# Second expert's output product in seven products for the three middle token blocks

## The chip, the core and the metric

The kernel runs on one core of a Trainium2 chip. The metric is the device time of one execution in microseconds (us).

## What is computed

Attention with a decay over 4 x 8 heads (576 tokens, 64 wide), then two experts, one after the other, on all 2304 tokens of width 512. The change lies in the last line of the second expert.

```python
def _moe2_ref(x, w_gate, w_val, w_out):          # x: 2304 x 512
    gate = 1.0 / (1.0 + np.exp(-(x @ w_gate)))   # w_gate, w_val: 512 x 1536
    val = x @ w_val
    return (gate * val @ w_out).astype(np.float32)   # w_out: 1536 x 512
```

## The kernel before

Every matrix is held as two float16 halves, a high and a low one, and a product A B is three matmuls on TensorE: high x high, high x low, low x high, summed in float32 in PSUM.

The second expert works on blocks of tokens, `XB` (L376): four of 512 and one of 256. Within a block there are six units (`units`, NJ = 6), each for 256 of the 1536 hidden columns. A unit does the following, all in `gv_stream` (L1379), which issues the TensorE work in a fixed order written out by hand.

- Gate and value together are one matrix product with seven products instead of eight, the form of Strassen and Winograd. `product` (L1356) issues one of them: 12 matmuls of half a block, 256 columns (128 in the last block). Four PSUM banks A, B, C, D hold the sums. `copy` (L1373) has ScalarE carry the running sum of A over to B, then to C, then to D.
- VectorE and ScalarE turn the banks into z = gate x value: `tanh`, `value2`, `first` and `second` (L1450 to L1481). `z_pair` (L1483) writes z in two float16 halves into a tile `zz`. The units' z comes in two float32 tiles, `t1` (two token quarters) and `v2`.
- The output product of unit u is `out_parts(u)` (L1493): one part for each 128 tokens, 6 matmuls of 512 columns. The parts are put into four slots of unit u + 1 (`some(slot)`, L1407): slot 0 after product t3, slot 1 after b21, slot 2 after t4, slot 3 after b22. They sum over the six units of the block in four PSUM banks (`o_acc`), and `store` (L1531) scales each to SBUF on ScalarE and sends it out.

The weights come as 64-bit floats. `conv` (L1298) loads and converts them to float32 on VectorE, `group` (L1241) makes the sums for the seven products, and `pair` and `out_pair` split them in halves. `sums(blk)` (L1312) makes the four sums of the token matrix that the seven products need. All this runs while the first expert ends and block 0 of the second one runs.

The order on each engine comes from the planner `Order` (L60). Each task is a generator that yields the engine and an estimate of the time; the planner issues the earliest that can start, and among those ready the one with the smallest due time. `take` and `give` hand out buffers, `need` waits for events. `scaled`, `rest` and `add` let the planner pick among VectorE, ScalarE and GpSimd. N1 = 72 is the number of the first expert's steps; unit u is due at N1 + 2.7 u.

Of the kernel before, what the change touches and what calls it, by code (L numbers as in the profile page):

```python
# [59 lines left out]
class Order:  # L60
# [242 lines left out]
def t_dve(cols):  # L303
    return cols * 1.04e-3 + 0.066
# [15 lines left out]
def attention_moe_moe_kernel(ctx, tc, qk, v, f, carry, ident, const, rows_q, rows_k, w_in, w_out, w_gate, w_val, w_out2, out):  # L320
# [26 lines left out]
        "d": 3, "r": 2, "g": 4, "e": 2,  # L347
        "sp": 4, "pp": 3, "pt": 5, "stage": 4, "vt": 4, "sm": 6, "low": 2, "q": NQ,
        "wr": 3, "wf": 2, "wr2": 2, "wf2": 6,
    }  # L350
# [19 lines left out]
    def t_g(name):  # L370
        return mt.tile([128, 2, 512], FP16, tag="g", name=name, bufs=BUFS["g"])
# [9 lines left out]
    def words(t, o, n):  # L381
        return t.rearrange("p a b c -> p (a b c)")[:, o:o + n]
# [793 lines left out]


    w2, f2, zz_t, s_t = {}, {}, {}, {}
    GDUE = 19.133
    GGAP = 2.2  # L1180
    NJ = NG2
# [16 lines left out]
    def w2_stream():  # L1198
        yield from need(*[("x", NB - 1, p, 1) for p in range(NPB)])
        done("att")  # L1200
        od.fill = None
        att.close()
        pool = ctx.enter_context(tc.tile_pool(name="w2", bufs=1))
        s_pool.append(pool)
        s0 = pool.tile([128, 4, 2, 512], FP16, name="s0")
        s_t[0] = [s0[:, i] for i in range(4)]

        old = [(t, key, g) for g in range(NG1) for t, key in ((win[g], "in"), (wout[g], "out"))]
# [24 lines left out]
        s_t[1] = [place("s1") for i in range(4)]  # L1233
        spawn(sums(0), N1 - GDUE)
        for j in range(NJ):
            where = {free[k] for k in free if k[1] == j and k != "s1"}
            spawn(group(j, pool, 6 * j, where), N1 - GDUE + GGAP * j)

    PIECES = ("b11", "t1", "b22", "t3", "t2", "b21", "t4")

# [51 lines left out]
    def out_pair(j, a, where):  # L1292
# [2 lines left out]
        yield from pair(w2["o", j][a], f2[f][0], S_WO2, ("w", "o", j, a))  # L1295
        give("wf2", f2[f][1])

    def conv(pool, src, key, n):  # L1298
        (ri,) = yield from take("wr2", turn=("wr2", n))
        raw = pool.tile([128, 512, 2], I32, tag="wr", name="wraw", bufs=BUFS["wr2"])  # L1300
# [5 lines left out]
        w = pool.tile([128, 512], I32, tag="wf", name="wf", bufs=BUFS["wf2"])  # L1306
        yield from float32(w, raw)
        give("wr2", ri)
        f2[key] = w.bitcast(FP32), fi
        done(key)  # L1310

    def sums(blk):  # L1312

        half = XB[blk] // 2
        n = 2 * half
        x = xt[blk]
        yield from need(*[("y", bb, h) for bb in range(2 * blk, 2 * blk + n // 256) for h in range(2)])
        if blk == 1:
# [7 lines left out]
        fis = yield from take(*["wf2"] * 4, turn=("wf2", blk and 6 * NJ + blk))  # L1326
        for q, fi in zip(("21", "22", "11", "12"), fis):
            w = s_pool[0].tile([128, 512], I32, tag="wf", name="af", bufs=BUFS["wf2"]).bitcast(FP32)[:, 0:n]
# [12 lines left out]
            if q == "12":  # L1341
                yield from add(f["12"][0], f["12"][0], f["11"][0], ALU.subtract, n)
                spawn(s_pair(s[3], f["12"][0], n, ("s", blk, 4)), due)
        for i, q in ((3, "21"), (2, "11"), (1, "22"), (4, "12")):
            yield from need(("s", blk, i))
            give("wf2", f[q][1])
# [7 lines left out]
    s_pool = []  # L1354

    def product(bank, piece, j, x, half, start):  # L1356

# [21 lines left out]
    def gv_stream():  # L1379
# [8 lines left out]
        outs = iter(())  # L1388
        for u, (blk, j) in enumerate(units):
            od.due(N1 + 2.7 * u)  # L1390
            done(("step", N1 + u))
            half = XB[blk] // 2
            n = 2 * half
            A, B, C, D = (t[:, 0:n] for t in banks)
            ntt = XB[units[u - 1][0]] // 128 if u else 0
# [10 lines left out]

            def some(slot):  # L1407

                if 4 - slot <= ntt:
                    part = next(outs, None)  # L1410
                    if part is not None:
                        yield from part()
# [27 lines left out]
            yield from need(("ad", u), ("s", blk, 4))  # L1440
            yield from product(D, "b22", j, s[3], half, False)
            spawn(first(u, t1, di, D, n), N1 + 2.7 * u - 30)
            if j == NJ - 1:
                done(("used", blk))
            yield from some(3)
            outs = iter(out_parts(u))
        for part in outs:
            yield from part()

    def tanh(u, t1, B):  # L1450

# [10 lines left out]
    def first(u, t1, di, D, n):  # L1462
        yield from need(("t", u))
        yield "DVE", t_dve(n)
        nc.vector.scalar_tensor_tensor(t1, t1, 1.0, D, op0=ALU.add, op1=ALU.mult)
        done(("z", u))
        yield from z_pair(u, 0, t1, n)
        give("d", di)

    def second(u, v2, ri, C, e, ei, n):  # L1470
        yield from need(("v", u))
        yield "DVE", t_dve(n)
        nc.vector.tensor_tensor(e, C, e, op=ALU.add)
        done(("g", u))
        yield "ACT", t_act(n), "exp"
        nc.scalar.activation(out=e, in_=e, func=ACTF.Tanh, scale=0.5 / (S_Y * S_GT))
        yield "DVE", t_dve(n), "port"
        nc.vector.scalar_tensor_tensor(v2, e, 1.0, v2, op0=ALU.add, op1=ALU.mult)
        give("e", ei)
        yield from z_pair(u, 1, v2, n)  # L1480
        give("r", ri)  # L1481

    def z_pair(u, h, z, n):  # L1483
        (gi,) = yield from take("g")
        zz = t_g("zz")
        yield from scaled(zz[:, 0, 0:n], z, S_ZS, n)
        yield from rest(zz[:, 1, 0:n], z, S_ZS, zz[:, 0, 0:n], n)
        zz_t[u, h] = (zz, gi)
        done(("zz", u, h))

    o_acc = {}
# [1 line left out]
    def out_parts(u):  # L1493
# [5 lines left out]
        def part(tt):  # L1499
# [4 lines left out]
            zz, gi = zz_t[u, h]  # L1504
            if j == 0:
                tag = f"acc{tt}" if tt < 2 else "s"
                (ai,) = yield from take(tag)
# [8 lines left out]
                nc.tensor.matmul(dst, lhsT=zh, rhs=w[:, 1], start=False, stop=False)  # L1516
                nc.tensor.matmul(dst, lhsT=zl, rhs=w[:, 0], start=False, stop=(j == NJ - 1 and ff == 1))  # L1517
            if t == ntt // 2 - 1:
                give("g", gi)
# [178 lines left out]
```

## Time and profile before

| | us |
|---|---|
| median of 3 runs | 927.55 |
| lowest and highest | 927.09, 931.93 |
| profiled execution | 930.57 |
| its span, first to last instruction | 928.8 |
| TensorE busy | 906.6 (98%) |
| VectorE busy | 628.1 (68%) |
| ScalarE busy | 520.0 (56%) |

Times in the rows are in us from the start of the span, and a duration named "mean ns" is in nanoseconds. Matmuls are pipelined: the listed duration of one reaches over the start of the next, so the pace is read from start to start. PE is TensorE (PEld its weight loads), DVE VectorE, ACT ScalarE, POOL GpSimd, SP the engine that issues most DMAs.

### The profile page before, as it was taken

To read this page: it belongs to the slowest core of one execution; us is meant where nothing else is said; L and a number is where in the kernel's file an instruction comes from. 1 tells how busy PE (TensorE), PEld (TensorE's weight loads), DVE (VectorE), ACT (ScalarE), POOL (GpSimd) and SP (SyncE) were. 2 spreads that over 40 slices of the span, in tenths; PEclk is the share of its full clock that TensorE was granted. 3 is DMA by queue.
4 is the path that set the end of the run, shared out by engine and by line. 5 is a ranking of instruction groups with operands and counts; after the bars stand their busy time and mean duration, and the time that the engine had idled before them with its cause. 6 is when DMAs were issued, how large, how long until landed. Compare 5 with 4: busy or idle time off the path is not lost.

```text
span 928.8 us, 20902 instructions
## 1 busy us (share of the span) xinstructions
PE 906.6 (98%) x8583; PEld 716.1 (77%) x8583; DVE 628.1 (68%) x1483; ACT 520.0 (56%) x994; POOL 34.6 (4%) x45
## 2 busy tenths in 40 slices
PE   8979989999999999999999999999999999999998
PEld 5647778787888878878888887777777777777776
DVE  6999988786768757787799999963236243442343
ACT  4768768897777769688444454544224322422232
POOL 0000100101000101000110000000000000000000
PEclk7979999999999999999999999999999999999999
DMA  8687995759457584546344443100000000100000
GB/s 234 163 210 200 231 230 142 132 115 182 99 111 125 107 172 88 114 81 109 103 141 138 154 137 114 46 13 35 2 1 35 13 1 1 47 1 1 13 35 24
DMA packets 145713, 90.50 MB, mean 97 GB/s; under 512 B 103657, under 2 KB 127681, under 8 KB 145616
## 3 DMA queue, kind: packets, MB, share of 16 engines
q1 hardware_dynamic: 144754, 87.85, 39.4%
q8 instruction: 67, 1.10, 0.5%
q10 hardware_dynamic: 864, 1.32, 0.4%
q14 instruction: 28, 0.23, 0.1%
HBM read 50.79 MB, written 4.84 MB: 60 GB/s over the span
## 4 chain that ended last, share of the span: by engine, by line
PE 75%; DVE 11%; ACT 5%; DMA 5%; SPq 2%; issue 2%; POOL 0%; ACTq 0%; POOLq 0%; DVEq 0%
PE bank L1369 9%; PE bank L1371 9%; PE bank L1370 9%; PE o_acc L1517 5%; PE o_acc L1516 5%; PE o_acc L1515 5%; PE y_ps L1131 5%; PE y_ps L1133 5%; PE y_ps L1132 5%; PE h_ps L1081 4%; PE h_ps L1083 4%; PE h_ps L1082 4%; PE o_ps L990 2%; DVE pp L731 2%; DMA pt<-pp 2%
## 5 line engine op out<-in xcount | busy, mean ns | idle before, releaser
L1131 PE MATMUL y_ps<-g,wout 128*128 128x256 f16 x576 | 157.3, 273 | 3.6 <-DVE xt L1163 2.1
L1082 PE MATMUL h_ps<-xt,win 128*128 128x256 f16 x576 | 156.9, 272 | 0.7 <-DVE sm L748 0.7
L1081 PE MATMUL h_ps<-xt,win 128*128 128x256 f16 x576 | 157.2, 273 | 0.2 <-DVE g L1054 0.2
L1132 PE MATMUL y_ps<-g,wout 128*128 128x256 f16 x576 | 157.0, 272 | 0.4 <-DVE wout L535 0.4
L1133 PE MATMUL y_ps<-g,wout 128*128 128x256 f16 x576 | 157.0, 272 | 0.0
L1083 PE MATMUL h_ps<-xt,win 128*128 128x256 f16 x576 | 156.9, 272 | 0.0
L1459 DVE TENSOR_TENSOR v<-bank,e 128x512 f32<-128x512 f32 (+1 forms) x30 | 19.1, 637 | 163.8 <-ACT bank L1376 163.6
L1376 ACT ACTIVATE bank<-bank 128x512 f32<-128x512 f32 (+1 forms) x90 | 48.5, 539 | 136.4 <-PE bank L1371 136.2
L731 DVE SCALAR_TENSOR_TENSOR pp<-sp,sm,pp 128x384 f16<-128x384 f32 (+4 forms) x128 | 78.3, 624 | 7.4 <-ACT pp L516 6.1
L723 DVE CUSTOM_DVE_ANT_0 sp<-s_ps,mask 128x384 f32<-128x384 f32 (+4 forms) x144 | 67.6, 492 | 16.6 <-PE s_ps L858 15.9
L873 ACT ACTIVATE sp<-sp,sm 128x384 f32<-128x384 f32 (+3 forms) x112 | 63.7, 569 | 20.8 <-DVE sm L723 19.8
L1081 PEld LDWEIGHTS <-win 128*128 128x128 f16 x576 | 56.3, 98 | 12.4 <-issue 1.4
L1132 PEld LDWEIGHTS <-wout 128*128 128x128 f16 x576 | 56.3, 98 | 12.2 <-issue 4.1
L1131 PEld LDWEIGHTS <-wout 128*128 128x128 f16 x576 | 56.3, 98 | 11.1 <-issue 2.0
L1082 PEld LDWEIGHTS <-win 128*128 128x128 f16 x576 | 56.3, 98 | 9.6 <-issue 1.3
L1083 PEld LDWEIGHTS <-win 128*128 128x128 f16 x576 | 56.3, 98 | 7.5 <-issue 0.8
L1133 PEld LDWEIGHTS <-wout 128*128 128x128 f16 x576 | 56.3, 98 | 6.6
L1054 DVE SCALAR_TENSOR_TENSOR g<-h_ps,g 128x512 f16<-128x512 f32 x72 | 48.9, 685 | 11.9 <-ACT g L1050 11.6
L1044 ACT ACTIVATE h_ps<-h_ps 128x512 f32<-128x512 f32 x72 | 41.7, 584 | 16.1 <-PE h_ps L1083 15.4
L990 PEld LDWEIGHTS <-vt 128*64 128x64 f16 x1368 | 36.3, 112 | 16.5 <-issue 13.2
L990 PE MATMUL o_ps<-pt,vt 128*64 128x128 f16 (+1 forms) x1368 | 44.8, 216 | 3.1 <-DMA pt<-pp 3.1
L516 ACT ACTIVATE pp<-sp,sm 128x384 f16<-128x384 f32 (+4 forms) x64 | 40.5, 644 | 9.5 <-ACT sp L873 3.0
(207 smaller groups left out, 2268.2 us busy)
## 6 DMA issues: line engine op xcount, KB each, us to landing
xt<-w_out SPq DMA_DIRECT2D x16, 512.0 KB
xt<-w_in SPq DMA_DIRECT2D x12, 512.0 KB
wraw<-w_gate SPq DMA_DIRECT2D x12, 512.0 KB
wraw<-w_val SPq DMA_DIRECT2D x12, 512.0 KB
wraw<-w_out SPq DMA_DIRECT2D x12, 512.0 KB
out<-ob SPq DMA_DIRECT2D x16, 256.0 KB
vst<-v SPq DMA_DIRECT2D x12, 320.0 KB
st<-qk SPq DMA_DIRECT2D x12, 320.0 KB
```

The lines of the kernel that those rows point to most:

```text
L723: nc.vector.tensor_tensor_reduce(out=sp, in0=ps_ap, in1=mk, op0=ALU.add, op1=ALU.min, scale=-0.125, scalar=1.0e38, accum_out=mn,)
L731: nc.vector.scalar_tensor_tensor(lo, a, scale, hi, op0=ALU.mult, op1=ALU.subtract)
L990: nc.tensor.matmul(o_ps[64 * hh:64 * hh + 64, col:col + n], lhsT=vv[:, jc, vl, 64 * hh:64 * hh + 64], rhs=ptt[:, k, q0:q0 + n], start=(jc ...
L1081: nc.tensor.matmul(dst, lhsT=wh, rhs=xh, start=(k == 0), stop=False)
L1082: nc.tensor.matmul(dst, lhsT=wh, rhs=xl, start=False, stop=False)
L1083: nc.tensor.matmul(dst, lhsT=wl, rhs=xh, start=False, stop=(k == KD - 1))
L1131: nc.tensor.matmul(dst, lhsT=wh, rhs=gh, start=first, stop=False, skip_group_check=True)
L1132: nc.tensor.matmul(dst, lhsT=wl, rhs=gh, start=False, stop=False, skip_group_check=True)
L1133: nc.tensor.matmul(dst, lhsT=wh, rhs=gl, start=False, stop=last, skip_group_check=True)
L1369: nc.tensor.matmul(dst, lhsT=wh, rhs=xh[:, k], start=first, stop=False, skip_group_check=True)
L1370: nc.tensor.matmul(dst, lhsT=wh, rhs=xl[:, k], start=False, stop=False, skip_group_check=True)
L1371: nc.tensor.matmul(dst, lhsT=wl, rhs=xh[:, k], start=False, stop=last, skip_group_check=True)
```

## The change

In blocks 1, 2 and 3 the output product is made for two units at a time, and in seven products instead of eight (Strassen and Winograd again). For one unit z is cut into 2 x 2 pieces (256 tokens by 128 hidden columns) and the output weights into 2 x 2 pieces (128 by 256). Each of the seven products is 12 matmuls of 256 columns: two units, two tiles of 128 tokens, three matmuls.

- `pieces` and `piece` make the eight pieces of a unit's z in float16 halves (A11, A12, A22 and the sums S1 to S4; A11 and A12 share a tile), in place of `z_pair`.
- `out_sums` makes the four sums of the weights (T1 to T4) of each unit in block 1. For the first four units T3 is written over the piece B12, which is first stored to DRAM (`b12_d`) and loaded back by `back` for block 4.
- `chain` issues the seven products p1, p7, p6, p2, p5, p4, p3 in seven slots: slots 1 to 3 of the unit after the pair, and slots 0 to 3 of the next. Four PSUM banks hold them; `copy` carries bank 0 to banks 1, 2 and 3 on ScalarE. `total` adds a bank to a float32 sum in SBUF, laid in the token tile of the block before, and with the block's last pair sends it out.
- Blocks 0 and 4 keep `out_parts`. In block 4 the parts of its units 0 and 1 move to its unit 2.
- `sums` of blocks 1 and up, and `out_sums`, wait until all weights are converted (`converted`). Buffers of the conversion become named slices (`f_t`, `raw_t`, `slots`).

The core of the diff:

```diff
+    def out_sums(j):
+        yield from converted()
+        w0, w1 = w2["o", j]
+        b12 = w0[:, :, 256:512]
+        if j < NSAVE:
+            yield "SP", 0.5, 128 * 1024
+            nc.sync.dma_start(out=b12_d[j], in_=b12)
+            done(("saved", j))
+        ia, ib = yield from take("wf3", "wf3")
+        f1, f2_ = (f_t[i % BUFS["wf3"]].bitcast(FP32) for i in (ia, ib))
+        yield from add(f1, w0[:, 0], w0[:, 1], ALU.add, 512)
+        yield from add(f2_, w1[:, 0], w1[:, 1], ALU.add, 512)
+        (a, b), (c, d) = ((f[:, 0:256], f[:, 256:512]) for f in (f1, f2_))
+        yield from add(a, b, a, ALU.subtract, 256)
+        yield from add(b, d, b, ALU.subtract, 256)
+        yield from add(d, d, a, ALU.subtract, 256)
+        yield from add(c, c, d, ALU.subtract, 256)
+        t = t_t[j]
+        if j < NSAVE:
+            yield from need(("part", j))
+            yield from pair2(b12, b, 1.0, 256)
+            yield from pair2(t[:, 0], a, 1.0, 256)
...
+    def pair2(dst, a, scale, n, *keys):
+        yield from scaled(dst[:, 0], a, scale, n)
+        yield "DVE", t_dve(n), "port"
+        nc.vector.scalar_tensor_tensor(dst[:, 1], a, scale, dst[:, 0], op0=ALU.mult, op1=ALU.subtract)
+        done(*keys)
...
+                if u < late:
+                    where = [(u + 1, k) for k in range(4)]
+                elif u < late + 2:
+                    where = [(late + 2, 2 * (u - late) + k) for k in range(2)]
+                else:
+                    where = [(u + 1, k) for k in (2, 3)]
+                at_slots(out_parts(u), *where)
+            elif j % 2:
+                at_slots(chain(u - 1, u), *[(u + 1, k) for k in (1, 2, 3)], *[(u + 2, k) for k in range(4)])
...
+    def pieces(u, t1, di, v2, ri):
...
+        yield from pair2(zz_t[u, "A22"][0], v2[:, 256:512], S_ZS, 256, ("zA22", u))
+        yield from need(("zt", u))
...
+        yield from pair2(za, t1, S_ZS, 512, ("zA11", u), ("zA12", u))
+        (a, b), (c, d) = ((f[:, 0:256], f[:, 256:512]) for f in (t1, v2))
+        yield from add(d, c, d, ALU.add, 256)
+        yield from add(c, a, c, ALU.subtract, 256)
+        yield from add(a, d, a, ALU.subtract, 256)
+        spawn(piece(u, v2, "S3", "S1", 0, 2, ("r", ri)), od.cur["due"])
+        yield from add(b, b, a, ALU.subtract, 256)
+        yield from piece(u, t1, "S2", "S4", 5, 7, ("d", di))
...
+        def product7(x, w, k, start):
+            bank = o_bank[k]
+            for u in us:
+                yield from after(("z" + x, u))
+                yield from need(("T", u % NJ))
+                z, buf = zz_t[u, x]
+                wp = wt[u % NJ][w]
+                yield "PE", t_pe(6, 256)
+                for t in range(2):
+                    dst = bank[:, t * 256:t * 256 + 256]
+                    zh, zl = (z[:, a, t * 128:t * 128 + 128] for a in range(2))
+                    first, last = start and u == u0 and t == 0, u == u1
+                    nc.tensor.matmul(dst, lhsT=zh, rhs=wp[:, 0], start=first, stop=False, skip_group_check=True)
+                    nc.tensor.matmul(dst, lhsT=zh, rhs=wp[:, 1], start=False, stop=False, skip_group_check=True)
+                    nc.tensor.matmul(dst, lhsT=zl, rhs=wp[:, 0], start=False, stop=last, skip_group_check=True)
...
+        def total(r, k, keys, done_, new=False, full=False):
+            yield from need(*keys)
+            if new:
+                yield "ACT", t_act(512, 0.05)
+                nc.scalar.activation(out=acc[:, r], in_=o_bank[k], func=ACTF.Copy, scale=1.0 / S_O)
+            else:
+                yield "DVE", t_dve(512)
+                nc.vector.scalar_tensor_tensor(
+                    acc[:, r], o_bank[k], 1.0 / S_O, acc[:, r], op0=ALU.mult, op1=ALU.add
+                )
...
+        def p1():
...
+            yield from product7("A11", "B11", 0, True)
+            spawn(copy(o_bank[1], o_bank[0], [("bank", 1, u0 - 1)], ("oab", u1)), -100)
+        def p7():
+            yield from need(("bank", 3, u0 - 1))
+            yield from product7("S3", "T3", 3, True)
+            done(("t3", u1))
+            tot(3, 3, (), (("ode", u1),), new=begin)
+            tot(2, 3, (), (("odf", u1),), new=begin)
...
+    def back(j):
+        yield from need(("t3", (len(XB) - 2) * NJ + j // 2 * 2 + 1))
+        yield "SP", 0.5, 128 * 1024
+        nc.sync.dma_start(out=w2["o", j][0][:, :, 256:512], in_=b12_d[j])
+        done(("back", j))
```

p6, p2, p5, p4 and p3 follow the same pattern: S2 T2 on bank 0, A12 B21 on bank 1, S1 T1 on bank 0, A22 T4 on bank 2, S4 B22 on bank 3; six totals in all for a pair.

## Rows read from the trace of the kernel before

**Rows 1.** The page: the span, and busy time of each engine

```profile
span 928.8 us, 20902 instructions
PE 906.6 (98%) x8583; PEld 716.1 (77%) x8583; DVE 628.1 (68%) x1483; ACT 520.0 (56%) x994; POOL 34.6 (4%) x45
```

**Rows 2.** View by windows: stretch, its length, each engine's busy us, granted clock, DMA

```profile
528.50:546.00 17.50, 17.50 (x160) 15.40 (x158) 17.08 (x31) 10.69 (x18) 0.00 (x0) 1.00 0.45 148
546.05:876.13 330.08, 330.08 (x2487) 243.05 (x2484) 164.46 (x274) 118.50 (x204) 1.04 (x1) 1.00 0.08 27
876.13:925.02 48.89, 48.89 (x601) 37.45 (x599) 20.14 (x52) 16.49 (x41) 0.00 (x0) 1.00 0.06 23
...
540.00:560.00 20.00, 20.00 (x164) 15.82 (x163) 19.59 (x35) 12.74 (x21) 0.00 (x0) 1.00 0.41 133
```

**Rows 3.** Timeline, TensorE, first matmuls in units 1 and 2: start us, duration us

```profile
546.05 0.27 PE L1369 MATMUL bank<-xt,b 128*128 128x256 f16 x1
...
547.36 0.27 PE L1369 MATMUL bank<-s,t 128*128 128x256 f16 x1
...
548.67 0.38 PE L1515 MATMUL o_acc<-wo,zz 128*128 128x512 f16 x1
...
549.96 0.27 PE L1369 MATMUL bank<-s,t 128*128 128x256 f16 x1
...
560.40 0.27 PE L1369 MATMUL bank<-xt,b 128*128 128x256 f16 x1
```

**Rows 4.** Weight loads by line, 610 to 876 us: count, busy us, mean ns

```profile
L1516 PEld LDWEIGHTS <-zz 128*128 128x128 f16 x150 | 14.7, 98 | 9.7
```

**Rows 5.** Timeline, block 4, first matmuls of its second unit's products 2, 3, 4

```profile
886.67 0.22 PE L1369 MATMUL bank<-s,t 128*128 128x128 f16 x1
...
887.34 0.22 PE L1369 MATMUL bank<-s,t 128*128 128x128 f16 x1
...
888.01 0.22 PE L1369 MATMUL bank<-xt,b 128*128 128x128 f16 x1
```

**Rows 6.** Groups by line, 610 to 876 us: count, busy us, mean ns, idle before

```profile
L1376 ACT ACTIVATE bank<-bank 128x512 f32<-128x512 f32 x55 | 32.0, 582 | 115.1 <-PE bank L1371 115.1
L516 ACT ACTIVATE zz<-v 128x512 f16<-128x512 f32 x5 | 3.2, 630 | 2.3 <-DVE v L1478 2.3
L535 DVE SCALAR_TENSOR_TENSOR zz<-v,zz 128x512 f16<-128x512 f32 x19 | 13.1, 691 | 0.5
L519 DVE TENSOR_SCALAR zz<-v 128x512 f16<-128x512 f32 x14 | 6.0, 427 | 0.5
L1189 DVE TENSOR_TENSOR af<-af 128x256 f32<-128x256 f32 x3 | 1.3, 423 | 0.1
L1189 POOL TENSOR_TENSOR af<-af 128x256 f32<-128x256 f32 x1 | 1.0, 1038 | 322.7 <-DVE af L1189 322.7
```

**Rows 7.** Timeline, unit 0 (no output parts): products 2 and 3, and ScalarE

```profile
530.87 0.27 PE L1369 MATMUL bank<-s,t 128*128 128x256 f16 x1
...
531.13 0.63 ACT L516 ACTIVATE wout<-wf 128x512 f16<-128x512 f32 x1 [2.41 <-DVE wf L659]
...
531.67 0.58 ACT L1376 ACTIVATE bank<-bank 128x512 f32<-128x512 f32 x1
...
532.30 0.27 PE L1369 MATMUL bank<-s,t 128*128 128x256 f16 x1
```

**Rows 8.** Timeline, two VectorE operations of 512 columns, one behind the other

```profile
688.62 0.69 DVE L535 SCALAR_TENSOR_TENSOR zz<-v,zz 128x512 f16<-128x512 f32 x1
689.22 0.68 DVE L1465 SCALAR_TENSOR_TENSOR t<-t,bank 128x512 f32<-128x512 f32 x1
```

**Rows 9.** Timeline, VectorE: the last weight conversion and the first of block 1's sums

```profile
596.05 0.69 DVE L1195 SCALAR_TENSOR_TENSOR wout<-wf,wout 128x512 f16<-128x512 f32 x1
...
596.65 0.69 DVE L1189 TENSOR_TENSOR af<-xt 128x512 f32<-128x512 f16 x1
```

More of the change, by code (lines that the diff above doesn't have):

```diff
@@ L1233, in w2_stream @@
         s_t[1] = [place("s1") for i in range(4)]
+        z22.append(place("z22"))
+        z22.append(free["z22"])
         spawn(sums(0), N1 - GDUE)
         for j in range(NJ):
-            where = {free[k] for k in free if k[1] == j and k != "s1"}
+            where = {free[k] for k in free if k[1] == j and k not in ("s1", "z22")}
             spawn(group(j, pool, 6 * j, where), N1 - GDUE + GGAP * j)
+        for j in range(NJ):
+            spawn(out_sums(j), N1 + 2.7 * (NJ + j) - TDUE)
     PIECES = ("b11", "t1", "b22", "t3", "t2", "b21", "t4")
@@ L1387, in gv_stream, with at_slots @@
         done(*[(k, -1) for k in ("ab", "ad", "t", "z", "g", "v")])
-        outs = iter(())
+        plan = {}
+        for j in range(NSAVE):
+            spawn(back(j), N1 + 2.7 * ((len(XB) - 2) * NJ + j + 3))
+        def at_slots(parts, *where):
+            for part, k in zip(parts, where):
+                plan.setdefault(k, []).append(part)
         for u, (blk, j) in enumerate(units):
@@ L1407, in some @@
             def some(slot):
[L1409 to L1412, printed above, removed]
+                for part in plan.pop((u, slot), ()):
+                    yield from part()
             yield from need(("v", u - 1), ("ad", u - 1))
@@ L1445, in gv_stream @@
             yield from some(3)
-            outs = iter(out_parts(u))
-        for part in outs:
-            yield from part()
+            if u == NJ - 1:
+                spawn(grab(), -100)
+            if not in_seven(u):
+                late = len(units) - NJ
+                if u < late:
+                    where = [(u + 1, k) for k in range(4)]
+                elif u < late + 2:
+                    where = [(late + 2, 2 * (u - late) + k) for k in range(2)]
+                else:
+                    where = [(u + 1, k) for k in (2, 3)]
+                at_slots(out_parts(u), *where)
+            elif j % 2:
+                at_slots(chain(u - 1, u), *[(u + 1, k) for k in (1, 2, 3)], *[(u + 2, k) for k in range(4)])
@@ new lines, in gv_stream, with in_seven, grab @@
+        for k in sorted(plan):
+            for part in plan[k]:
+                yield from part()
+    def in_seven(u):
+        return 0 < units[u][0] and XB[units[u][0]] == 512
+    def grab():
+        yield from need(("zz", NJ - 1, 0), ("zz", NJ - 1, 1))
+        yield from take(*["g"] * 4)
+        zp["A1"] = [t_g("za") for i in range(3)]
+        zp["A22"] = [t[:, :, k:k + 256] for t in (z22[0], t_g("zb")) for k in (0, 256)]
+        done("grab")
+    def pieces(u, t1, di, v2, ri):
+        yield from need(("zv", u), z22[1], "grab")
+        (i,) = yield from take("A22")
+        zz_t[u, "A22"] = zp["A22"][i % BUFS["A22"]], ("A22", i)
+        yield from pair2(zz_t[u, "A22"][0], v2[:, 256:512], S_ZS, 256, ("zA22", u))
+        yield from need(("zt", u))
+        (i,) = yield from take("A1")
+        za = zp["A1"][i % BUFS["A1"]]
+        zz_t[u, "A11"] = za[:, :, 0:256], ()
+        zz_t[u, "A12"] = za[:, :, 256:512], ("A1", i)
+        yield from pair2(za, t1, S_ZS, 512, ("zA11", u), ("zA12", u))
[6 more added lines that the diff above has]
+        yield from piece(u, t1, "S2", "S4", 5, 7, ("d", di))
@@ new lines, in piece, with chain, tot, p6 @@
+    def piece(u, f, p, q, kp, kq, buf):
+        ip, iq = yield from take(p, q)
+        i, k = kp + ip % BUFS[p], kq + iq % BUFS[q]
+        zz_t[u, p] = slots[0][:, i], (p, ip)
+        zz_t[u, q] = slots[0][:, k], (q, iq)
+        dst = slots[0][:, i:k + 1:k - i].rearrange("p i a n -> p a i n")
+        yield from pair2(dst, f.rearrange("p (i n) -> p i n", i=2), S_ZS, 512, ("z" + p, u), ("z" + q, u))
+        give(*buf)
+    def chain(u0, u1):
+        us = (u0, u1)
+        blk = units[u0][0]
+        begin, end = u0 % NJ == 0, u1 % NJ == NJ - 1
+        acc = words(xt[blk - 1], 0, 4096).bitcast(FP32).rearrange("p (r n) -> p r n", r=4)
+        def product7(x, w, k, start):
[13 more added lines that the diff above has]
+                    nc.tensor.matmul(dst, lhsT=zl, rhs=wp[:, 0], start=False, stop=last, skip_group_check=True)
+                if buf:
+                    give(*buf)
+        def total(r, k, keys, done_, new=False, full=False):
[3 more added lines that the diff above has]
+                nc.scalar.activation(out=acc[:, r], in_=o_bank[k], func=ACTF.Copy, scale=1.0 / S_O)
+            else:
+                yield "DVE", t_dve(512)
+                nc.vector.scalar_tensor_tensor(
+                    acc[:, r], o_bank[k], 1.0 / S_O, acc[:, r], op0=ALU.mult, op1=ALU.add
+                )
+            done(*done_)
+            if full and end:
+                t0 = blk * 512 + 256 * (r // 2)
+                yield "SP", 0.5, 128 * 2048
+                nc.sync.dma_start(
+                    out=out[t0:t0 + 256, 256 * (r % 2):256 * (r % 2) + 256].rearrange("(a p) n -> p a n", p=128),
+                    in_=acc[:, r].rearrange("p (a n) -> p a n", a=2),
+                )
+        def tot(*a, **k):
+            spawn(total(*a, **k), -100)
+        def p1():
+            if "tag" not in o_bank:
+                tags = ("acc0", "acc1", "s", "s")
+                ais = yield from take(*tags)
+                o_bank.update(enumerate(t_ps(tag, "o_bank") for tag in tags))
+                o_bank["tag"] = list(zip(tags, ais))
+                done(*[("bank", k, u0 - 1) for k in range(4)], ("oad", u0 - 1))
+            yield from need(("bank", 0, u0 - 1), ("oad", u0 - 1))
+            yield from product7("A11", "B11", 0, True)
[6 more added lines that the diff above has]
+            tot(2, 3, (), (("odf", u1),), new=begin)
+        def p6():
+            yield from need(("oab", u1))
+            yield from product7("S2", "T2", 0, False)
+            spawn(copy(o_bank[2], o_bank[0], [("bank", 2, u0 - 1)], ("oac", u1)), -100)
+        def p2():
+            yield from product7("A12", "B21", 1, False)
+            tot(0, 1, (), (("bank", 1, u1),), new=begin, full=True)
+        def p5():
+            yield from need(("oac", u1))
+            yield from product7("S1", "T1", 0, False)
+            spawn(copy(o_bank[3], o_bank[0], [("ode", u1), ("odf", u1)], ("oad", u1)), -100)
+            tot(3, 0, [("ode", u1)], (("bank", 0, u1),), full=True)
+        def p4():
+            yield from product7("A22", "T4", 2, False)
+            tot(2, 2, [("odf", u1)], (("bank", 2, u1),), full=True)
+        def p3():
+            yield from need(("oad", u1))
+            yield from product7("S4", "B22", 3, False)
+            tot(1, 3, (), (("bank", 3, u1),), new=begin, full=True)
+            if end and units[u1 + 1][0] == len(XB) - 1:
+                spawn(release(u1), -100)
+        return [p1, p7, p6, p2, p5, p4, p3]
@@ L1450, in tanh, with release @@
+    o_bank = {}
+    def release(u):
+        for k, (tag, ai) in enumerate(o_bank["tag"]):
+            yield from need(("bank", k, u), ("oad", u))
+            give(tag, ai)
+    def back(j):
[3 more added lines that the diff above has]
+        done(("back", j))
     def tanh(u, t1, B):
@@ L1465, in first @@
         nc.vector.scalar_tensor_tensor(t1, t1, 1.0, D, op0=ALU.add, op1=ALU.mult)
-        done(("z", u))
-        yield from z_pair(u, 0, t1, n)
-        give("d", di)
+        done(("z", u), ("zt", u))
+        if not in_seven(u):
+            yield from z_pair(u, 0, t1, n)
+            give("d", di)
     def second(u, v2, ri, C, e, ei, n):
@@ L1479, in second @@
         give("e", ei)
-        yield from z_pair(u, 1, v2, n)
-        give("r", ri)
+        done(("zv", u))
+        if not in_seven(u):
+            yield from z_pair(u, 1, v2, n)
+            give("r", ri)
     def z_pair(u, h, z, n):
-        (gi,) = yield from take("g")
-        zz = t_g("zz")
+        if u < NJ:
+            (gi,) = yield from take("g")
+            zz, buf = t_g("zz"), ("g", gi)
+        else:
+            tag, k = (("S4", 7), ("S1", 2))[h]
+            (gi,) = yield from take(tag)
+            zz, buf = slots[0][:, k + gi % BUFS[tag]], (tag, gi)
         yield from scaled(zz[:, 0, 0:n], z, S_ZS, n)
         yield from rest(zz[:, 1, 0:n], z, S_ZS, zz[:, 0, 0:n], n)
-        zz_t[u, h] = (zz, gi)
+        zz_t[u, h] = (zz, buf)
         done(("zz", u, h))
@@ L1503, in part @@
             yield from need(("w", "o", j, 0), ("w", "o", j, 1))
-            zz, gi = zz_t[u, h]
+            if blk and j < NSAVE:
+                yield from need(("back", j))
+            zz, buf = zz_t[u, h]
             if j == 0:
@@ L1518, in part @@
             if t == ntt // 2 - 1:
-                give("g", gi)
+                give(*buf)
+            if blk == 0 and tt == ntt // 2 - 1:
+                done(("part", j))
             if j == NJ - 1:
```

49 lines of the change are left out of this document (41 added, 8 removed).

## The prediction

> **What bounds the kernel now.** I read the page first: one engine fills the span, TensorE, with VectorE far behind it [rows 1]. A share over the whole span mixes stages, so next I cut the second expert out with the view by windows. From the first product of its first unit to its last output matmul TensorE is busy for every microsecond of each stretch, at a granted clock of 1.00 (the 2.4 GHz level), while VectorE has about half of the middle stretch free [rows 2]. The view of TensorE's waits has no entry at all after 500 us. So in this stage a microsecond of matmul time taken away is a microsecond of run time, as long as what feeds TensorE keeps up. The change takes matmuls away here and nowhere else, so the question is pace and supply.
>
> The pace comes from the timeline of TensorE [rows 3]. A gate or value product (12 matmuls of 256 columns) goes from 546.05 to 547.36, 1.31 us, or 0.109 us for each matmul. An output part (6 matmuls of 512 columns) goes from 548.67 to 549.96, 1.29 us; over a unit the parts come to 1.295 on average: 560.40 - 546.05 = 14.35 us for seven products and four parts, and (14.35 - 7 x 1.31) / 4 = 1.295. The listed duration of a matmul (0.27, 0.38) is not its price; start to start is.
>
> **The change, part by part.**
>
> **Matmuls.** By the diff a pair of units in blocks 1 to 3 gives up 8 parts and gets 7 products, each 2 units x 2 token tiles x 3 = 12 matmuls of 256 columns. Removed: 8 x 1.295 = 10.36 us. Added: 7 x 1.31 = 9.17 us. That is 1.19 us a pair, and with nine pairs 10.7 us. Blocks 0 and 4 keep their parts; only their places move, so they cost the same.
>
> **Weight loads.** Each 256-column matmul still has a load of its own: 84 in a pair where there were 48. A load takes 98 ns [rows 4], less than the 109 ns of the matmul that covers it, and the same alternation runs at 0.109 in every gate product, so I price the loads at nothing. If that cover were gone, the change would lose from 10.36 / 84 = 0.123 us a matmul on, 14 ns more than now. The Trainium skill (TensorE: Matmul & The Clock Gate, Back-to-back issue gap) speaks against the change: it gives 131 ns for a 512-column matmul with its load and 81 ns for one of 128 columns. An estimate from it for 256 columns is 98 ns, so a pair would go from 48 x 0.131 = 6.3 to 84 x 0.098 = 8.2 us, a loss of 17 us over nine pairs. The trace disagrees with that page: it has 0.215 at 512 columns [rows 3] and 0.67 us for twelve of 128, or 0.056 each [rows 5].
>
> **Bank copies and the empty slots.** The new chain copies bank 0 to banks 1, 2 and 3 (ScalarE, 0.58 us [rows 6]), and each copy has at least one product of another kind, 1.31 us, between its source and its reader, so it hides. What gets thinner is the old chain. Four output parts a unit used to stand between its products; now slot 0 of the unit after each pair is empty, and unit 7 has no part at all. That makes 9 + 3 further places with only one product of cover (slot 3 of unit 7, the fourth, is counted with VectorE below). Two stretches show the price. Unit 0 has no parts: there a conversion on ScalarE stood ahead of the copy, the copy ran 531.67 to 532.25, and the third product began at 532.30 instead of 530.87 + 1.31 = 532.18, 0.1 us lost [rows 7]. In block 4 the products are half as long, slots 0 and 1 are empty, and the third and fourth follow without a gap [rows 5]. So 0 to 12 x 0.11 = 1.3 us; I take 0.5, because ScalarE has room most of the time [rows 2] and only meets such a conversion now and then.
>
> **VectorE.** By durations [rows 6], a unit of blocks 1 to 3 will have: four operations on gate and value, 4 x 0.69; the remainders of the pieces, 3 x 0.69 + 0.42; their first halves, at most 4 x 0.43, or on ScalarE at 0.63; four piece sums of 256, 4 x 0.42 (on GpSimd 1.04); three totals, 3 x 0.69; and a sixth of the next block's twelve sums, 1.38. That is 12.1 us with everything on VectorE, 10.4 with the first halves on ScalarE, against 7 x 1.31 + 3.5 x 1.31 = 13.76 us of TensorE. Durations overstate it: start to start 0.60 stands against 0.69 [rows 8]. So it fits and lies beside TensorE, and I cost it at nothing. VectorE at 98% did not hold TensorE up either: 19.59 of 20 us, with TensorE at 20.00 [rows 2]. Urgent work goes first there, because totals, copies and unit work are due earlier than the sums of weights. The piece deadlines are wide too: the first Strassen product of a pair comes slot 3 plus four products (6.55 us) after the unit that it needs, and the two operations, one total and one leftover in between are about 3 us. Into block 4, with short products, it is 1.31 + 4 x 0.67 = 4.0 us, still enough. After unit 7, z has only the next product's 1.31 us; one VectorE operation in its way would cost about 0.3 us, once.
>
> **Weight sums, block 1.** Each of six groups: two adds of 512 and four of 256 (3.06 us), remainders (1.5), first halves (1.3): 5.9, together 35 us. The last must be ready before slot 1 of unit 12. The conversions end and block 1's own sums begin where they do now, at 596 [rows 9], so the new wait for all conversions moves the latter little, and they end at about 606. Unit 6 begins at 546.05 + 5 x 14.35 = 617.8; then 14.35 (unit 6), 9.17 (unit 7), 13.1, 14.41, 13.1, 14.41 (units 8 to 11) and four products give 701.6. That leaves 95 us. The demand is 35 + 3.6 (unit 5) + 6 x 12.1 = 111 at worst, and at the pace of 0.60, with the first halves on ScalarE, (27 + 3 + 6 x 10.4) x 0.87 = 81. So the cost is 0 to 15 us; I take 0, since rows 8 are VectorE's own pace and ScalarE has more than half of its time free [rows 2].
>
> **DMAs and queues.** SP gets four stores of B12 (128 KB each), four loads back and 12 output stores in place of 12. DMA is busy for 0.08 of the middle stretch [rows 2]. The write of T3 over B12 waits for the store; behind it on its queue (VectorE or ScalarE) stand bank copies. The store is issued before six adds (3 us), so I take 0; a microsecond of wait, four times, bounds it at 4. The loads back follow block 3's T3 products and have whole units until block 4's parts. The tail is the last unit of block 4, untouched.
>
> **Sum.** 10.7 - 0.5 = 10.2 us. The profiled execution took 930.57 us (span 928.8) and would come to 920.4; it lies 3.0 above the median of the runs, 927.55, from which I forecast 917.4.
>
> **The rivals.** (1) The weight sums are late: unit 12 waits once. For it: 111 against 95. Against: the pace. Price 2 to 15 us: 919 to 932. (2) A wait in every pair, for a piece or a copy, eats the gain: 0.5 to 1.2 us nine times, 922 to 928. Against it: slots without cover that ran gapless [rows 5]. (3) Slower: VectorE becomes the bound in blocks 1 to 3. It decides from 14.35 us a unit (13.76 to cancel nothing). My high sum is 12.1, so every one of some 19 instructions would need a further 0.15 us of waiting: 15.0 a unit, 18 x (15.0 - 14.35) = +12, about 939. (4) Slower: weight loads stick out. It decides from 0.123 us a matmul; with a quarter of a load (25 ns) uncovered, 84 x 0.134 - 10.36 = 0.9 a pair, +8, about 935. The Trainium skill's section named above is the rule for this one; the pace at both lengths speaks against it. (5) The change does not do what it says (fewer columns): the count is plain in the code, I give it nothing.
>
> **How the numbers follow.** Forecast 0.80; (1) 0.09, two thirds of it still a gain; (2) 0.03; (3) 0.05; (4) 0.03. About 0.5%, 4.6 us, is what a measurement of this kernel can tell from no change. Faster by more: 0.80 + 0.06 = 0.86. Within it: 0.03 + 0.03 = 0.06. Slower: 0.08. The range runs from 915.6 (all 10.7 us and the lowest of the runs, less about a microsecond of spread) to 922.5 (the store's four microseconds or a short case of (1) on top); it leaves out about 0.15.
>
> **What would show it.** After: TensorE without waits from 530 to the end; 12 new matmuls in 1.31 us; a unit of blocks 1 to 3 in about 13.76 us, so block 4 starts some 10 us earlier; VectorE at 65 to 85% there. Wrong would be: waits of TensorE for pieces or totals on VectorE, a gap at slot 1 of unit 8 or 12, or a pace above 0.11 in the new products.

## The result

| | before | after |
|---|---|---|
| median of 8 runs, us | 929.32 | 921.83 |
| lowest to highest, us | 927.09 to 933.25 | 918.23 to 923.73 |
| profiled execution, us | 930.57 | 918.23 |
| its span, us | 928.8 | 916.4 |
| second expert's stage, us | 395.24 | 385.39 |

The ratio of the times is 0.9906, with a 95% interval of 0.9879 to 0.9933: 8.7 us less, between 6.2 and 11.2. The stage in the last row runs from the first matmul of the second expert's first product to the start of its last output matmul (529.56 to 924.80 before, 526.79 to 912.18 after). It is the measure of most of what follows, because it does not hold the scatter of the attention stage.

The page of the kernel after, span and engines, answers to [rows 1]:

```profile
span 916.4 us, 21847 instructions
PE 898.3 (98%) x8907; PEld 750.3 (82%) x8907; DVE 708.0 (77%) x1655; ACT 572.1 (62%) x1100; POOL 42.3 (5%) x48
```

TensorE's busy time fell by 8.3 us although it has 324 more matmuls; VectorE's rose by 80 us and ScalarE's by 52. Hardly any of that shows in the time, and the view by windows says why (after; the columns of [rows 2]; first block 1, but for a microsecond at its start, then block 2):

```profile
616.00:695.00 79.00, 78.36 (x693) 67.53 (x691) 61.32 (x117) 46.33 (x86) 1.99 (x1) 1.00 0.04 15
...
694.46:777.00 82.54, 82.54 (x759) 73.98 (x757) 55.08 (x96) 42.93 (x78) 4.08 (x2) 1.00 0.04 14
```

In block 2 TensorE has no gap, and VectorE is busy for 67% of the time. In block 1 TensorE is without a listed matmul for 0.64 us. The pace of the new products is in the timeline of TensorE (after, block 2: the block's first matmul, the first matmul of a new product, the first of the gate product behind it, and block 3's first):

```profile
694.46 0.27 PE L1440 MATMUL bank<-xt,b 128*128 128x256 f16 x1
...
699.70 0.27 PE L1599 MATMUL o_bank<-win,za 128*128 128x256 f16 x1
...
701.01 0.27 PE L1440 MATMUL bank<-s,t 128*128 128x256 f16 x1
...
776.99 0.27 PE L1440 MATMUL bank<-xt,b 128*128 128x256 f16 x1
```

A new product takes 701.01 - 699.70 = 1.31 us, as the gate products do [rows 3], and six units take 82.53 us: 13.76 a unit, where it was 14.35.

Two waits are all that is left between 500 us and the end. The view of TensorE's waits lists the larger (engine and line, what it waited for, us in total, times, longest):

```profile
PE o_bank L1601 <- DVE room L1362: 0.5, 1, 0.5
```

From start to start this product, the second of the first pair, took 1.97 us instead of 1.31: 0.66 lost. The other is 0.31 us in unit 7, which the view does not list. The rows around both (after, timeline of all engines):

```profile
636.27 0.63 ACT L517 ACTIVATE room<-t 128x512 f16<-128x512 f32 x1 [0.25 <-DVE t L1194]
...
636.81 0.58 ACT L1447 ACTIVATE bank<-bank 128x512 f32<-128x512 f32 x1
...
637.02 0.27 PE L1442 MATMUL bank<-xt,t 128*128 128x256 f16 x1
...
637.44 0.27 PE L1440 MATMUL bank<-wout,b 128*128 128x256 f16 x1
...
646.54 1.99 POOL L1194 TENSOR_TENSOR room<-room 128x512 f32<-128x512 f32 x1 [180.56 <-DVE room L1194]
...
647.92 0.89 DVE L1194 TENSOR_TENSOR t<-t 128x256 f32<-128x256 f32 x1
...
648.74 0.68 DVE L1362 SCALAR_TENSOR_TENSOR room<-v,room 128x512 f16<-128x512 f32 x1
...
649.47 0.28 PE L1601 MATMUL o_bank<-wo,room 128*128 128x256 f16 x1 [0.49 <-DVE room L1362]
```

In unit 7 ScalarE first made half of a piece, which itself waited for VectorE, and only then the bank copy that the next product needed. At the first pair the last piece of S3 came late from VectorE: one add of 256 columns took 0.89 us, where such adds take 0.42 [rows 6], and a GpSimd operation ran over the same time. So the stage adds up: 395.24 - 10.71 (nine times 8 x 1.295 - 7 x 1.31) + 0.97 (the two waits) - 0.11 (unit 0's gap of [rows 7], which is gone) = 385.39, as measured.

### The profile page after: what moved, and what is told of

It is laid out like the page before. It is cut to its first block, busy times and chain, and to the rows that moved or that the text cites. A ratio compares the mean times of both kernels' runs of the same rounds, so it can differ in the third digit from the quotient of the medians.

```text
span 916.4 us, 21847 instructions
## 1 busy us (share of the span) xinstructions
PE 898.3 (98%) x8907; PEld 750.3 (82%) x8907; DVE 708.0 (77%) x1655; ACT 572.1 (62%) x1100; POOL 42.3 (5%) x48
## 4 chain that ended last, share of the span: by engine, by line
PE 75%; DVE 12%; DMA 5%; ACT 5%; issue 2%; SPq 1%; POOL 0%; ACTq 0%; POOLq 0%; DVEq 0%
PE bank L1440 8%; PE bank L1442 8%; PE bank L1441 8%; PE y_ps L1132 5%; PE h_ps L1082 5%; PE y_ps L1134 5%; PE y_ps L1133 5%; PE h_ps L1084 5%; PE h_ps L1083 5%; PE o_bank L1601 3%; PE o_bank L1599 3%; PE o_bank L1600 3%; PE o_ps L991 3%; DMA pt<-pp 3%; DVE pp L732 2%
## 5 line engine op out<-in xcount | busy, mean ns | idle before, releaser
L1132 PEld LDWEIGHTS <-wout 128*128 128x128 f16 x576 | 56.3, 98 | 11.2 <-issue 2.0
L1613 DVE SCALAR_TENSOR_TENSOR xt<-o_bank,xt 128x512 f32<-128x512 f32 x42 | 28.4, 689 | 34.8 <-ACT o_bank L1447 25.5
```

The lines of the kernel that those rows point to most:

```text
L1132: nc.tensor.matmul(dst, lhsT=wh, rhs=gh, start=first, stop=False, skip_group_check=True)
```

## The experiments

My theory was that the gain is matmul time on TensorE and that the rest is hidden. Its rivals: waits set the pace of the new chain; weight loads stick out at 256 columns; VectorE or its place in the chain costs.

| kernel | stage, us | gaps of TensorE in it, us |
|---|---|---|
| before | 395.24 | 0.11 |
| after | 385.39 | 0.97 |
| an eighth product | 396.50 | 0.31 |
| before, parts in 256 columns | 397.03 | 0.21 |
| sums three units later | 384.81 | 0.41 |
| sums off GpSimd | 384.90 | 0.49 |
| four operations ahead of the pieces | 396.97 | 12.61 |
| eight ahead | 437.99 | 53.61 |
| 16 small ones beside | 395.90 | 11.41 |
| 28 beside | 424.15 | 39.7 |
| both remedies | 384.72 | 0.31 |
| and halves off ScalarE | 385.19 | 0.82 |

A gap is the time from the first matmul of a product or part to the first of the next, less the number of matmuls times their pace (0.1092, 0.2157 or 0.0558 us); with 28 beside, time lost within the last part is added. Each stage is read from one profile. Block 0 is the same in all kernels with the change and took 88.12 or 88.13 us in each of them but one (sums three units later, 88.22), so differences of a few tenths can be read.

Three of the gaps are not waits alone. In the runs with four and eight operations ahead and with 28 beside, the granted clock fell to 0.50 (the 1.2 GHz level) for some microseconds after TensorE had stood waiting. Matmuls of 256 columns then follow each other in 0.213 us instead of 0.109. That makes up 2.7, 7.4 and 4.4 us of the gaps in these three. In the other runs the clock stayed at 1.00 through the stage.

**An eighth product.**

```diff
         def p1():
...
-            yield from product7("A11", "B11", 0, True)
+            for again in range(2):
+                yield from product7("A11", "B11", 0, True)
```

> The changed kernel with one product of the new chain issued twice (A11 B11, the second overwrites the first), so eight products a pair again, everything else as it is: 12 more matmuls of 256 columns in each of nine pairs. The stage, from the first product matmul of the second expert to the start of the last output matmul, took 395.24 us before and 385.39 after. Theory (the gain is TensorE time and nothing else): 385.4 + 9 x 1.31 = 397.2, so about 2 us slower than the kernel before. Rival (waits on VectorE or ScalarE set the pace of the new chain, TensorE has slack): the added matmuls fit into waits, 385.4 to 390.

The stage took 396.50 us, 11.1 more than the changed kernel's; nine products are 11.8, and the wait at the first pair (0.66) is gone, since the doubled product gives the piece time. The whole time was 1.0015 of the kernel before's (0.9994 to 1.0036), where the stage alone would give 1.3 us, 1.0014. With its eighth product back, the new form gains nothing: the gain is TensorE's time. The rival, that added matmuls fit into waits, is out.

**Smaller matmuls in the kernel before.**

```diff
-                nc.tensor.matmul(dst, lhsT=zh, rhs=w[:, 0], start=(j == 0 and ff == 0), stop=False)
...
+                for c in (0, 256):
+                    d, w0, w1 = dst[:, c:c + 256], w[:, 0, c:c + 256], w[:, 1, c:c + 256]
+                    first, last = j == 0 and ff == 0 and c == 0, j == NJ - 1 and ff == 1
+                    nc.tensor.matmul(d, lhsT=zh, rhs=w0, start=first, stop=False, skip_group_check=True)
+                    nc.tensor.matmul(d, lhsT=zh, rhs=w1, start=False, stop=False, skip_group_check=True)
+                    nc.tensor.matmul(d, lhsT=zl, rhs=w0, start=False, stop=last, skip_group_check=True)
```

> The kernel before with every output matmul of 512 columns made as two of 256, each with its own weight load: 648 matmuls more, the same columns. Theory (a load of 98 ns stays hidden below a 256-column matmul): 648 x (2 x 0.1092 - 0.2157) = 1.7 us, stage 395.2 -> 397. Rival (the loads stick out; a quarter of one, 25 ns, uncovered): 1296 x 0.025 = 32 us more, about 429. The estimate from the Trainium skill (TensorE: Matmul & The Clock Gate, Back-to-back issue gap), 98 ns for 256 columns against 131 for 512, stands by itself: 648 x (2 x 98 - 131) ns = 42 us more.

The stage took 397.03 us, 1.8 more; the ratio was 1.0021 (0.9992 to 1.0049). The timeline of a part (first matmul of the part, and of the product behind it):

```profile
700.75 0.27 PE L1518 MATMUL o_acc<-win,zz 128*128 128x256 f16 x1
...
702.06 0.27 PE L1369 MATMUL bank<-xt,b 128*128 128x256 f16 x1
```

Twelve half-width matmuls with twelve loads take 1.31 us, where six full ones took 1.295. Halving a matmul from 512 columns costs 2.7 ns each, not a load. Rival (4) is out, and with it the loss that the Trainium skill's pace (TensorE: Matmul & The Clock Gate, Back-to-back issue gap) would have meant. The trace disagrees with that pace at both lengths for which the section gives it: 215.7 ns against 131 at 512 columns, and 55.8 against 81 at 128. It does not disagree with all that this section of the Trainium skill states, as the prediction has it: the gap given there for a single matmul of N columns, N / 2.4 + 2.5 ns, is the pace of this trace at all three lengths.

**The wait at the first pair: two remedies.**

```diff
-                if blk + 1 < len(XB):
-                    spawn(sums(blk + 1), N1 + 2.7 * u + 4)
+            if j == (3 if blk else 0) and blk + 1 < len(XB):
+                spawn(sums(blk + 1), N1 + 2.7 * u + 4)
```

> The changed kernel with the token sums of blocks 2, 3 and 4 started three units later (in the fourth unit of the block before), nothing else. After the change TensorE lost 0.66 us at the second Strassen product of the first pair (waiting for the piece S3 of unit 7) and 0.31 in unit 7. Theory A (VectorE is crowded there by the sums of block 2, which the planner lets run as soon as they can): the 0.66 goes, stage 385.4 -> 384.7. Theory B (a GpSimd operation that ran beside VectorE stretched one VectorE add from 0.42 to 0.89 us): gone only if that operation moves too. Rival: the wait stays or moves to another place, 385.4 or more.

```diff
-        (plan,) = pick([("DVE", t_dve(n), "port")], [("POOL", t_pool(n))])
+        plans = [[("DVE", t_dve(n), "port")], [("POOL", t_pool(n))]]
+        (plan,) = pick(*plans[0:1 if ("T", 0) in od.event else 2])
```

> The changed kernel with the sums of the second expert kept off GpSimd once the first weight sums are made: four operations move to VectorE. Theory B (GpSimd's operation made the piece late): the 0.66 us wait goes, stage 384.7, no VectorE add above 0.7 us. Theory A (VectorE is crowded): the wait stays or grows, since VectorE gets more work, 385.4 to 386.

Later sums: 384.81, no gap at that product, but a new one of 0.10 us in unit 4. Off GpSimd: 384.90, and 0.18 of the 0.66 us stays there. So both theories hold a part: the GpSimd operation is one of the next block's sums, so moving the sums takes away both it and the crowd on VectorE, while moving GpSimd's work to VectorE leaves some of the crowd. Both together:

> The changed kernel with both remedies of the wait at the first pair: the token sums of blocks 2 to 4 start three units later, and the second expert's sums stay off GpSimd once the first weight sums are made. Each alone brought the stage from 385.39 to 384.8 or 384.9. Theory (one wait, two remedies): 384.7 to 384.9 again, not less; the 0.31 us of unit 7 stays. The whole time, if the stage's 10.4 us are all that differs: ratio 0.9888 to the kernel before; if the changed kernel's stage before the second expert were slower too, nearer to the 0.9906 measured for it.

384.72, inside the expected range, and only the 0.31 of unit 7 left. This version is at 0.9895 of the kernel before (0.9855 to 0.9936). It beats the kernel before; against the changed kernel its 0.67 us in the stage is too little for the times to tell.

**The wait in unit 7.** The same version, with the first halves of the pieces of units 6 and 7 on VectorE instead of where the planner puts them:

```diff
+        if act:
+            yield from scaled(dst[:, 0], a, scale, n)
+        else:
+            yield "DVE", t_dve2(n), "port"
+            nc.vector.tensor_scalar(dst[:, 0], a, scale, 0.0, op0=ALU.mult, op1=ALU.add)
```

> The version with both remedies (stage 384.72), and besides the first halves of the pieces of units 6 and 7 on VectorE alone, so that none of them stands on ScalarE ahead of a bank copy. The one wait left, 0.31 us at the last product of unit 7, came behind a piece's half on ScalarE that itself waited for VectorE; with VectorE loaded more (four operations a unit) the same place lost 4.5 us. Theory (ScalarE's queue is the cause): the wait goes, stage 384.4. Rival (VectorE is simply late there): it stays at 0.3 or grows, or a wait for a piece comes at the first pair, 384.7 to 386, since VectorE gets some 1.7 us more in each of the two units.

The stage grew to 385.19. The copy's wait went, but the next product, the first of unit 8, began 0.14 us late, right behind an operation of unit 7 on VectorE (`value2`):

```profile
637.06 0.68 DVE L1702 TENSOR_TENSOR v<-bank,e 128x512 f32<-128x512 f32 x1
...
637.80 0.27 PE L1445 MATMUL bank<-xt,b 128*128 128x256 f16 x1
```

The product behind that lost 0.68 us, and is in the view of waits:

```profile
PE bank L1445 <- DVE t L1708: 0.5, 1, 0.5
```

That is z of unit 7, which has only one product of cover since slot 3 of unit 7 is empty. My theory was half right: ScalarE's queue did pass VectorE's lateness on, but taking the work to VectorE costs more there. The rival holds.

**VectorE's room, ahead of the pieces.**

```diff
         yield from need(("zt", u))
+        for _ in range(4):
+            yield "DVE", t_dve(512), "port"
+            nc.vector.scalar_tensor_tensor(t1, t1, 1.0, t1, op0=ALU.mult, op1=ALU.max)
         (i,) = yield from take("A1")
```

> The changed kernel with four more VectorE operations of 512 columns (0.60 us each, they leave the value as it is) in every unit of blocks 1 to 3, placed in the chain of a unit's pieces, ahead of A11, A12 and all that follows: the pieces come 2.4 us later. From the prediction the first Strassen product has 6.55 us and needs about 3, so 3.5 us are free. Theory (wide deadlines): stage 385.4 to 386.5, no more than the first pair's wait grows. Rival (2) of the prediction (a wait in each pair): nine waits of 0.5 us or more, 390 or more.

The stage took 396.97 us. My forecast of 385.4 to 386.5 failed as a sum and held in place: blocks 2 and 3 lost 0.44 us between them, with VectorE busy for 69.08 of block 2's 82.96 us. Units 7 and 8 lost 9.7, and block 4 lost 2.5 at its first new products (1.08 and 1.39 us). The view of waits names the largest, and the timeline shows why (ScalarE's rows with VectorE's ahead):

```profile
PE bank L1440 <- ACT bank L1447: 4.3, 1, 4.3
```

```profile
641.26 0.42 DVE L1194 TENSOR_TENSOR t<-t 128x256 f32<-128x256 f32 x1
641.59 0.68 DVE L1362 SCALAR_TENSOR_TENSOR room<-v,room 128x512 f16<-128x512 f32 x1
641.71 0.63 ACT L517 ACTIVATE room<-t 128x512 f16<-128x512 f32 x1 [1.25 <-DVE t L1194]
...
642.25 0.58 ACT L1447 ACTIVATE bank<-bank 128x512 f32<-128x512 f32 x1
```

It is the small wait of the changed kernel grown: the piece's half waits on ScalarE for VectorE, and the bank copy stands behind it. Of the 9.7 us, 2.7 are not waits but the clock. After the 4.3 us without work the next two products had a granted clock of 0.50 (view by windows, the last number but two); the first of them took 645.39 - 642.88 = 2.51 us instead of 1.31 (timeline):

```profile
642.88:647.95 5.07, 5.07 (x25) 3.60 (x24) 4.96 (x10) 2.51 (x5) 0.00 (x0) 0.50 0.14 52
```

```profile
642.88 0.37 PE L1440 MATMUL bank<-wout,b 128*128 128x256 f16 x1 [4.30 <-ACT bank L1447]
...
645.39 0.42 PE L1440 MATMUL bank<-xt,b 128*128 128x256 f16 x1
```

Eight such operations:

> The same with eight: the pieces come 4.8 us later, about 1.3 more than the 3.5 us that are free, and VectorE has 4.8 us more in each unit. Theory (the piece deadline decides): a wait of 1 to 1.5 us in each of nine pairs, stage 395 to 399, the gain gone. Rival (VectorE's time decides, not the place of the work): 55.1 us in six units of block 2 is 9.2 a unit by durations, about 8 by pace, and 8 + 4.8 = 12.8 is still below 13.76, so 385.4 to 387, the same as for the run with as much VectorE work beside the chain.

437.99 us, 53.6 of them gaps, 7.4 of these the lower clock. 9.6 us went at the copy in unit 7. At the first product of a pair TensorE lost 3.0 to 3.4 us for the first pair of a block, 1.4 for the second, and 5.5 to 9.2 for the last, whose products run in the next block. The forecast of 1 to 1.5 us (the added time less the free time) thus held for three pairs of nine, and neither theory had the sum. The deadline decides more than VectorE's time: the view of waits gives 27.1 us in nine waits to the piece A11, while VectorE itself stood idle for 33 of the 290 us of blocks 1 to 3. Why the other pairs lose so much more was not tried; the sums of the next block run beside the last pair's products.

**VectorE's room, beside the pieces.** The added operations are on a tile of their own, due later than all else, and the sums and halves stay off GpSimd from there on as far as the planner's choice goes.

```diff
+    def idle_work(n):
+        for _ in range(n):
+            yield "DVE", t_dve(200)
+            nc.vector.tensor_tensor(junk[0], junk[0], junk[0], op=ALU.add)
...
                 spawn(pieces(u, t1, di, v2, ri), N1 + 2.7 * u - 30)
+                spawn(idle_work(16), N1 + 2.7 * u + 10)
```

> The changed kernel with 16 more VectorE operations of 200 columns (some 0.27 us each by pace, 4.3 us in all, on a tile of their own) in every unit of blocks 1 to 3, due later than all else, and the second expert's sums and halves kept off GpSimd from there on. VectorE then has about 8 + 4.3 = 12.3 us of 13.76 in a unit. Theory (VectorE costs nothing until it is full, urgent work first): 384.9 to 386.5. Rival (each operation in the way of an urgent one costs, since none is broken off): about 0.1 us at each of a dozen places a pair, 10 us, 395.

> The same with 28 operations: 7.6 us more, about 15.6 us of VectorE against 13.76 of TensorE in a unit. Theory (rival 3 of the prediction: from 13.76 us a unit VectorE is the bound): 18 units x 1.8 = about 33 us longer, stage 410 to 425, VectorE busy 95% or more in blocks 1 to 3. Against it: if late work may slide into block 4, where VectorE has room, or durations overlap more than thought, less: 386 to 400.

With 16 the stage took 395.90 us, and the rival was right (395). In the window that is block 2 in the changed kernel (here it begins 4 us before block 2 and ends 10 us before its end), VectorE was busy for 80.25 us, 97%, and TensorE for 77.97:

```profile
694.46:777.00 82.54, 77.97 (x704) 68.62 (x703) 80.25 (x192) 38.51 (x71) 0.00 (x0) 1.00 0.04 14
```

By the view of waits 7.0 us went in seven waits for z (in units 10 to 13, 15, 16 and 20, for the z of the unit before), and the timeline shows the late work ahead of the urgent (VectorE, and the product that waited):

```profile
740.83 0.69 DVE L1723 TENSOR_TENSOR e<-bank,e 128x512 f32<-128x512 f32 x1
741.43 1.16 DVE L1267 TENSOR_TENSOR junk<-junk 128x200 f32<-128x200 f32 x3
742.51 0.69 DVE L1728 SCALAR_TENSOR_TENSOR v<-e,v 128x512 f32<-128x512 f32 x1
743.11 0.76 DVE L1267 TENSOR_TENSOR junk<-junk 128x200 f32<-128x200 f32 x2
743.79 0.68 DVE L1714 SCALAR_TENSOR_TENSOR t<-t,bank 128x512 f32<-128x512 f32 x1
...
744.52 0.27 PE L1450 MATMUL bank<-s,wout 128*128 128x256 f16 x1 [1.43 <-DVE t L1714]
```

The order was fixed when the program was built. Work that the planner put into a pause of VectorE stays in front of z when there is no pause left. With 28 the stage took 424.15 us, the upper end of what full occupation gave (410 to 425). That it fits is in part luck: blocks 1 to 3, for which the forecast had 33 us, lost 20.8, and block 4, into which 190 of the 504 added operations slid, lost 18.9. So VectorE is free at 67% and at 83%, and costs about a microsecond a pair at 97%.

## Why the prediction was right

The forecast was 917.4 us, 10.2 less than a median of 927.55; measured were 8.7 less by the ratio, and 921.83 against a before of 929.32. Step by step:

- **What bounds.** Right. A microsecond of TensorE taken away in this stage was a microsecond, and one given back cost as much (the eighth product).
- **Matmuls.** 10.7 us forecast. The stage gives 9.85 + 0.97 - 0.11 = 10.71.
- **Weight loads.** Nothing, as forecast; shown by the halved matmuls and by 1.31 us a product.
- **Copies and empty slots.** 0.5 us forecast, 0.31 measured, at one of the twelve places and by the mechanism named, another ScalarE operation ahead of the copy. Nine slots without a part (slot 0 after each pair) cost nothing.
- **VectorE.** 10.4 to 12.1 us a unit by durations was too high: those of block 2 add up to 58.98, 9.8 a unit (busy time, in which overlaps count once, 55.08 / 6 = 9.2). Four totals of a block ran on ScalarE and two of its sums on GpSimd. That it costs nothing on the path was right in blocks 2 and 3, with room up to 83%. That urgent work goes first, so that even 98% is no harm, was the weak reason: with 16 operations beside, at 97%, 11 us were lost.
- **Piece deadlines.** For the normal pairs wide, as forecast (2.4 us more cost 0.44 in two blocks). For block 4 I had 4.0 against about 3, a microsecond free; 2.4 more should then wait 1.4, and the first new product there waited 1.08, the second another 1.39. The second Strassen product of the first pair was not in my list; it is where 0.66 was lost.
- **Weight sums.** No wait, but the working was off. I set 81 to 111 us of VectorE against 95 of time and so gave a rival 0.09. The last T half (VectorE, after) was done 62 us before its product at 699.70:

```profile
636.76 0.68 DVE L1362 SCALAR_TENSOR_TENSOR wraw<-room,wraw 128x512 f16<-128x512 f32 x1
```

The step that failed counted all the unit work up to unit 12 as standing ahead of the sums; the planner runs them as soon as it can, while units 5 and 6 leave room. What they may have cost is in the crowd around unit 7, where both waits lie; a kernel without them was not tried.
- **DMAs.** The stores of B12 were issued by 584 us, and the first write over B12 came at 607.86 (the first half, on ScalarE); no wait.
- **Block 4's start.** It came 13.8 us earlier in the stage, not some 10: the products of the last pair run in block 4, whose time up to its last part grew from 47.6 to 51.6 us. The sign that I named, 18 units at 13.76 instead of 14.35, counts every pair's products into its own block.
- **The level.** 4.4 us above the forecast, and 0.7 below the top of the range, though the stage is within 0.4 us of it. The base carried 1.8 of the difference: the median of the kernel before was 927.55 in three runs, 929.32 in eight and 929.52 in nineteen. The rest lies in what the median gained: 7.5 of the stage's 9.85. So the sum is right by its mechanism, and that the time itself stayed in the range has some luck in it. The interval of the ratio (6.2 to 11.2) holds 9.85; that the two differ by more than chance is not shown.

## What to carry to other kernels

Price a matmul by start to start, not by its listed duration: where TensorE has no gap, seven products of half-width matmuls against eight parts of full ones can be worked out to a tenth of a microsecond. Ask of each engine that takes the extra work not whether it has room on average but where the crowd is: here every wait lay in the two units in which one-time work (weight sums, the next block's sums) met the first new pieces. An in-order engine hands its lateness on, so look at what stands behind an operation that waits, above all the short copies that TensorE needs.

## What the runs showed of the hardware that was not expected

- GpSimd's sum of 256 columns took 1.04 us in the kernel before [rows 6], 2.65 after, and 0.73 and 0.75 with four operations ahead, a run with a fuller VectorE; its sums of 512 took 1.60 to 2.52 after. So a fuller VectorE alone does not set the time; what does was not tried. A VectorE add that ran beside one took 0.89 us instead of 0.42, and two with four operations ahead 1.37 and 1.26. Keeping the sums off GpSimd brought back 0.49 us, though it gave VectorE more work.
- A wait of TensorE can cost more than its length: after 4.3 us without work (four operations ahead) the granted clock was 0.50 for the products behind it, and 2.7 us more were lost.
- The order of instructions on every engine up to the second expert is the same in the kernels before and after, yet the second expert began at 529.56 us in one profile and 526.79 in the other; over the profiles of this case it began between 526.02 and 531.41. That is as much scatter as half of the gain, all of it from the attention stage and the first expert. What makes it was not tried.
